# Attending the first and last batch in half-heads, with the half-batch MLPs woven in sooner and q/k loaded apart from v

## The chip, the cores and the metric

One core of a Trainium2 chip runs the kernel. The metric is the device time in microseconds (us) of one execution; "median" is over several executions. The span of a profile runs from the first to the last instruction of the program and is about 1.8 us shorter than the time of the same execution. TensorE is called PE in the profile, VectorE DVE, ScalarE ACT, GpSimd POOL, SyncE SP. SP issues most of the DMAs.

## The reference, cut to what matters

Hashed attention over 4 batches, 8 heads, 768 positions, 64 features, followed by an MLP:

```python
q_bits = einsum('bhsd,dk->bhsk', q, proj) > 0      # 6 bits; k_bits likewise
mask   = bucket(q_bits)[..., :, None] == bucket(k_bits)[..., None, :]
scores = where(mask, q @ k.T / sqrt(64), -1e9)
attn   = softmax(scores)
x      = (attn @ v).transpose(0, 2, 1, 3).reshape(3072, 512)
h      = x @ w_in                  # 512 -> 2048
out    = (h * cos(h)) @ w_out      # 2048 -> 512
```

The kernel puts 6 features of +0.5 or -0.5 for the hash bits behind the 64 features of q and k, so that one matmul gives score and mask together, and the exp of a score with differing bits vanishes.

## The kernel before

A *slot* is one head. In slot `hd`, nine *units* run; each makes 512 of the 4608 score columns of head `hd` and a ninth of the attention of head `hd - 1`. Between the units stand the preparation of later heads and, from slot 12 on, the MLP of a finished batch.

```python
for hd in range(NH + 1):
    for i in WEIGHTS.get(hd, ()):
        load_weight(i)                       # POOL issues; 16 loads in slots 3 to 12
    if hd in MLP_AT:                         # {12: 0, 20: 1, 28: 2}
        for c in range(2):
            hidden(MLP_AT[hd], c, wide)      # x @ w_in, sin on ACT, product on DVE
    for u in range(NU):                      # NU = 9
        scores(hd, u)                        # PE, then exp on ACT
        attend(hd - 1, u * NA, (u + 1) * NA) # PE
        ...                                  # project(): pieces of g @ w_out; plan: preparation
    normalize(hd - 1)                        # DVE: reciprocal and product into xtok
    if hd % H == 0:
        for t in range(SB):
            to_features(hd // H - 1, t)      # SP: DMA transpose of xtok into xT
...                                          # tail: rest of batch 2's MLP, the whole of batch 3's
```

Preparing a head takes a load of q, k and v (SP, two heads at a time), six transposes (PE) with two evictions, two casts to bf16 (DVE), and the hash: a matmul with `proj` for up to four heads at once, a threshold on DVE, and two small DMAs per head that place the bits in the rows behind the features. In the profile's lines `nat` (later `nat_qk` and `nat_v`) is a loaded pair, `ext` the features with their bits, `xtok` the attention's result, `xT` the same transposed, `win` and `wout` the two weight matrices, and the `L` number a line of that run's kernel.

```python
def place_bits(heads, bits):
    for j, hd in enumerate(heads):
        for r in range(2):
            a = 32 * j + r * NBITS
            nc.sync.dma_start(out=e_all[D:KEXT, hd % NE, :, r * HB:(r + 1) * HB],
                              in_=bits[a:a + NBITS])
...
for m in range(4, NH // 2):
    at(2 * m - 7, 2, load_pair, m)           # slot, unit: load of heads 2m, 2m+1
...
    if hd % GH == GH - 2 and hd + 2 < NH and hd > 2:
        hash_at(hd, 5, list(range(hd + 2, hd + 2 + GH)))   # then place_bits of four heads
```

The softmax here doesn't subtract the row's maximum and nothing guards it: scores larger than these inputs give would overflow.

## Time and profile before

| | before |
|---|---|
| time, median (runs) | 335.7 us (335.0 to 336.5, 4 runs) |
| span of the profile | 333.1 us |
| TensorE work, back to back (worked out below) | 302.9 us |
| first exp / first hidden layer / last exp ends | 10.7 / 75.9 / 276.5 us |
| ACT table loads | 8 of 1.28 us |

The page's first two parts: busy time of each engine, and the span in 40 slices of 8.3 us (a digit is the busy share in tenths; PEclk is the granted TensorE clock).

```profile
PE 320.3 (96%) x2794; PEld 193.6 (58%) x2794; DVE 175.8 (53%) x346; ACT 243.6 (73%) x453; POOL 82.4 (25%) x219
...
PE   7889999799999999999999999999999999999995
...
ACT  3677989689788768869778868869878882577211
...
PEclk9999999799999999999999999999999999999999
DMA  7943784999601405565000515341000003500021
```

PE is the limit, but its busy share does not say by how much, because the record of a matmul overlaps those of its neighbours (a record of 512 columns lasts 378 ns, and the next matmul starts after 216). So I took for each shape of matmul the usual distance from one start to the next in dense stretches (512 columns 216 ns, 384 columns 162 ns, 65-column attend about 30 ns, fp32 transpose 109 ns, a pass of a hash group 330 ns) and added these up. That gives 302.9 us of work; the other 30.2 us of the span are lost. They lie as follows, by the start of each reciprocal, which ends a slot: 12.3 us up to the end of slot 6, at 49.2 us; 6.3 us in slots 7 to 11; 7.6 us from there to the end of attention; 4.1 us in the tail. The split is good to about 1 us: a second working, with slightly different spacings, gave 13.1, 6.4, 6.3 and 4.2 us.

The one large hole is near 60 us. The windows view gives busy time in chosen stretches: length, then PE, weight loads, DVE, ACT, POOL, with the granted clock, the DMA share and GB/s last.

```profile
core 0: us, PE busy (x) PEld busy (x) DVE busy (x) ACT busy (x) POOL busy (x), PEclk, DMA share, GB/s
...
46.00:53.00 7.00, 7.00 (x88) 4.41 (x87) 4.43 (x9) 5.99 (x13) 3.28 (x10) 1.00 0.44 88
53.00:62.00 9.00, 6.89 (x85) 5.00 (x83) 5.20 (x11) 7.70 (x16) 5.41 (x14) 1.00 0.80 195
62.00:66.30 4.30, 4.08 (x34) 2.90 (x35) 0.76 (x3) 2.60 (x5) 0.28 (x1) 0.60 1.78 174
66.30:76.00 9.70, 9.70 (x126) 6.59 (x125) 6.72 (x13) 8.57 (x18) 7.26 (x17) 1.00 0.91 204
```

PE stands for 2 us before 62 us, and then runs at 0.60 of its clock in the mean. What it waits for is the first row of the next answer (waits view: who waited for whom, total us, times, longest):

```profile
PE tp L123 <- DMA nat<-in_k_dram: 2.3, 1, 2.3
```

And this is why that load came late (timeline of SP's queue: start, length, operation):

```profile
37.35 0.41 SPq L82 DMA_DIRECT2D nat<-in_q_dram  x1
...
49.00 6.24 SPq L169 DMA_DIRECT2D ext<-bits  x8
55.36 0.37 SPq L82 DMA_DIRECT2D nat<-in_q_dram  x1
```

The eight bit placements of one hash group hold SP for 6.24 us, 0.78 us each, and the load of pair 7 stands behind them in program order.

### The profile page before, as it was taken

How to read it: one execution, taken by the hardware profiler on the slowest of the kernel's cores; microseconds unless marked ns; L12 is line 12 of the kernel's file. 1: busy time of each engine (PE TensorE's matmuls, PEld its weight loads, DVE VectorE, ACT ScalarE, POOL GpSimd, SP SyncE). 2: the span in 40 equal slices, each digit the busy share in tenths (PEclk: the TensorE clock that was granted, in tenths of full speed). 3: DMA queues.
4: the chain of work that ended last, by engine and by line, in shares of the span. 5: the costliest groups of instructions: out<-in, count | busy, mean ns of one | idle time of the engine just before them, and what ended most of it. 6: DMA issues, size and time to landing. Idle time of an engine off the chain costs nothing.

```text
span 333.1 us, 7151 instructions
## 1 busy us (share of the span) xinstructions
PE 320.3 (96%) x2794; PEld 193.6 (58%) x2794; DVE 175.8 (53%) x346; ACT 243.6 (73%) x453; POOL 82.4 (25%) x219
## 2 busy tenths in 40 slices
PE   7889999799999999999999999999999999999995
PEld 2466767565666566656666656656565565566442
DVE  6787766376884444554885444352983101188100
ACT  3677989689788768869778868869878882577211
POOL 9993645376002223222002222221000000000000
PEclk9999999799999999999999999999999999999999
DMA  7943784999601405565000515341000003500021
GB/s 209 321 136 91 175 242 100 210 224 179 177 3 38 148 31 176 96 211 174 6 1 2 175 36 176 69 94 43 0 1 2 33 31 81 143 2 1 33 94 63
DMA packets 34398, 33.55 MB, mean 101 GB/s; under 512 B 15060, under 2 KB 30396, under 8 KB 34364
## 3 DMA queue, kind: packets, MB, share of 16 engines
q1 hardware_dynamic: 30732, 28.76, 29.5%
q0 software_dynamic: 3328, 4.20, 8.1%
q8 instruction: 22, 0.36, 0.5%
q10 hardware_dynamic: 304, 0.13, 0.1%
q14 instruction: 12, 0.10, 0.1%
HBM read 27.27 MB, written 6.29 MB: 101 GB/s over the span
## 4 chain that ended last, share of the span: by engine, by line
PE 82%; ACT 7%; DVE 4%; DMA 3%; issue 3%; POOL 1%; SPq 0%; ACTq 0%; DVEq 0%
PE y L307 18%; PE st L201 16%; PE st L283 13%; PE o_att L283 9%; PE o_att L230 9%; PE tp L307 6%; PE tp L123 5%; ACT pt L209 5%; PE tp L155 4%; DMA nat<-in_k_dram 3%; DVE ext L142 1%; PE o_att L220 1%; ACT o_sb L322 1%; DVE ext L147 1%; ACT L291 1%
## 5 line engine op out<-in xcount | busy, mean ns | idle before, releaser
L209 ACT ACTIVATE pt<-st 128x512 f16<-128x512 f32 x288 | 158.8, 610 | 37.1 <-PE st L201 35.2
L201 PE MATMUL st<-ext 128*128 128x512 bf16 (+1 forms) x384 | 108.2, 328 | 1.5 <-ACT pt L209 1.3
L230 PEld LDWEIGHTS <-pt 128*128 128x128 f16 x1152 | 72.3, 98 | 39.1 <-issue 1.4
L307 PE MATMUL y<-wout,gt 128*128 128x512 f16 x288 | 89.3, 378 | 0.8
L230 PE MATMUL o_att<-v_ext,pt 128*128 128x65 f16 x1152 | 82.7, 195 | 0.3 <-ACT pt L209 0.3
L107 POOL CAST v_ext<-nat 128x192 f16<-128x192 f32 x64 | 21.8, 368 | 138.4 <-PE o_att L230 135.9
L201 PEld LDWEIGHTS <-ext 128*128 128x128 bf16 x384 | 36.8, 98 | 23.6 <-issue 10.6
L295 DVE TENSOR_TENSOR gt<-st,cs 128x384 f16<-128x384 f32 x76 | 41.9, 556 | 5.5
L291 ACT ACTIVATE cs<-st 128x384 f16<-128x384 f32 x76 | 37.2, 491 | 9.7 <-PE st L283 9.5
L307 PEld LDWEIGHTS <-gt 128*128 128x128 f16 x384 | 33.1, 98 | 18.2 <-issue 1.4
L295 DVE TENSOR_TENSOR gt<-o_att,cs 128x384 f16<-128x384 f32 x52 | 28.9, 557 | 21.2 <-ACT cs L291 17.8
L244 DVE RECIPROCAL rec<-o_att 128x6 f32<-128x6 f32 x32 | 6.3, 196 | 62.7 <-PE o_att L230 62.7
L123 PE MATMUL tp<-ident,nat 128*128 128x128 f32 x186 | 31.9, 282 | 3.9 <-DMA nat<-in_k_dram 2.3
L291 ACT ACTIVATE cs<-o_att 128x384 f16<-128x384 f32 x52 | 25.6, 492 | 6.4 <-PE o_att L283 6.3
L123 PEld LDWEIGHTS tp<-ident,nat 128*128 128x128 f32 x186 | 22.3, 143 | 9.9 <-issue 3.6
L283 PE MATMUL st<-xT,win_100 128*128 128x384 f16 x76 | 24.8, 326 | 0.0
L283 PE MATMUL st<-xT,win_101 128*128 128x384 f16 x76 | 24.8, 326 | 0.0
L283 PE MATMUL st<-xT,win_102 128*128 128x384 f16 x76 | 24.8, 326 | 0.0
L283 PE MATMUL st<-xT,win_103 128*128 128x384 f16 x76 | 24.8, 326 | 0.0
L307 PE MATMUL tp<-wout,gt 128*128 128x512 f16 x96 | 21.2, 379 | 0.0
L111 POOL TENSOR_TENSOR vacc<-nat 128x192 f32<-128x192 f32 x32 | 18.8, 589 | 0.0
L245 DVE TENSOR_TENSOR xtok<-o_att,rec 128x384 f16<-128x384 f32 x32 | 17.8, 557 | 1.6 <-DMA xT<-xtok 0.5
(173 smaller groups left out, 358.0 us busy)
## 6 DMA issues: line engine op xcount, KB each, us to landing
out_dram<-o_sb SPq DMA_DIRECT2D x23, 256.0 KB
nat<-in_q_dram SPq DMA_DIRECT2D x15, 384.0 KB
nat<-in_k_dram SPq DMA_DIRECT2D x15, 384.0 KB
nat<-in_v_dram SPq DMA_DIRECT2D x15, 384.0 KB
wout<-in_moe_w_out_dram POOLq DMA_DIRECT2D x8, 256.0 KB, 8.4
ext<-bits SPq DMA_DIRECT2D x62, 9.0 KB
win_100<-in_moe_w_in_dram POOLq DMA_DIRECT2D x2, 256.0 KB, 4.2
win_101<-in_moe_w_in_dram POOLq DMA_DIRECT2D x2, 256.0 KB, 6.8
```

The costliest lines, as they stand in the source:

```text
L107: nc.gpsimd.tensor_copy(out=dst[:, r], in_=src[:, r])
L111: nc.gpsimd.tensor_add(acc, x[:, 0:3 * D], x[:, 3 * D:6 * D])
L123: nc.tensor.matmul(out=tp[:, i * P:(i + 1) * P], lhsT=nat[hd][:, w, i * 2 * D:(i + 1) * 2 * D], rhs=ident, is_transpose=True, start=(i == ...
L155: nc.tensor.matmul(out=jp[32 * j:32 * (j + 1), 0:HB], lhsT=projx, rhs=f32[hd][:, w], start=True, stop=True,)
L201: nc.tensor.matmul(out=st[:, o:o + n], lhsT=e[:, 1, jt * P:(jt + 1) * P], rhs=e[:, 0, c:c + n], start=True, stop=True,)
L209: nc.scalar.activation(out=pts[hd][:, u * UNIT:(u + 1) * UNIT], in_=st, func=ACTF.Exp, bias=EXP_BIAS, scale=EXP_SCALE,)
L230: nc.tensor.matmul(out=o_ps[:, qt * VW:(qt + 1) * VW], lhsT=pts[hd][:, jt * S + qt * P:jt * S + (qt + 1) * P], rhs=v_all[:, hd % NV, jt], ...
L245: nc.vector.tensor_tensor(out=xtok[b][:, :, h * D:(h + 1) * D], in0=o_ps[:, :, 0:D], in1=rec.to_broadcast([P, SB, D]), op=ALU.mult,)
L283: nc.tensor.matmul(out=hp[:, 0:TOK], lhsT=win_t[ft][:, ff * P:(ff + 1) * P], rhs=xT[:, ft, b * S + c * TOK:b * S + (c + 1) * TOK], start=( ...
L291: nc.scalar.activation(out=cs, in_=hp[:, 0:TOK], func=ACTF.Sin, bias=math.pi / 2.0, scale=1.0)
L295: nc.vector.tensor_tensor(out=gt, in0=hp[:, 0:TOK], in1=cs, op=ALU.mult)
L307: nc.tensor.matmul(out=y_state[b, t], lhsT=gates[b, c][ff][:, tt * P:(tt + 1) * P], rhs=wout_t[:, ff], start=(ff == 0), stop=(ff == NFF - 1),)
```

## The change

Batch 0 and batch 3 are attended in half-heads: a slot then holds the even query rows of two heads instead of all rows of one. After five slots the even rows of all heads of batch 0 are done, so half a batch can go through the MLP: the first hidden layer moves from slot 12 to slot 7. In batch 3 the first half-batch is woven into the attention, and a shorter MLP is left at the end. q and k have a load and four buffers of their own, v another. The scores use the 70 filled rows and no longer the zeroed 128. The core of the diff, cut:

```diff
+    SLOTS = []
+    for b in range(B):
+        if 0 < b < B - 1:
+            SLOTS += [[(b * H + i, 0, SB)] for i in range(H)]
+        else:
+            first = [(b * H + i, 0, NQ) for i in range(H)]
+            rest = [(b * H + i, NQ, NQ) for i in range(H)]
+            if b == 0:
+                first.insert(1, rest.pop(0))
+            halves = first + rest
+            SLOTS += [halves[i:i + 2] for i in range(0, 2 * H, 2)]
...
-    MLP_AT = {12: 0, 20: 1, 28: 2}
...
+    hiddens.update({7: [(0, 0)], 10: [(0, 1)], 18: [(1, 0)], 19: [(1, 1)], 26: [(2, 0)], 27: [(2, 1)], 30: [(3, 0)]})
+    spread([(0, t) for t in range(SB)], 7, 18)
...
-        load_pair(0, 1)
+        load_qk(0, 1)
...
+        load_qk(1)
+        load_v(0)
+        load_qk(2)
+        load_v(1)
...
-    WEIGHTS = {3 + i: (i,) for i in range(8)}
-    WEIGHTS.update({11: (8, 9), 12: (10, 11, 12, 13, 14, 15)})
...
+    for i in range(8):
+        at(1.4 + 0.4 * i, load_weight, i)
+        at(5 + 0.25 * i, load_weight, 8 + i)
...
-    both(1, 2, transpose, 4)
...
+    hash_at(1.6, [4, 5])
...
+    hash_at(2.5, [6, 7])
...
+                if s == 5:
+                    attend(4, min(2 * u * NA, SB * SB), min(2 * (u + 1) * NA, SB * SB))
...
+                if s == 5 and u == SB * SB // (2 * NA):
+                    normalize(4)
+                    for t in range(NQ):
+                        to_features(0, t)
```

The last two pieces attend slot 4 at double pace inside slot 5 and then transpose the first half-batch by DMA, so that `xT` is there for the hidden layer of slot 7. The second weight matrix (`load_weight` 8 to 15, the tile `wout`) is asked for from slot 5 on.

More of the change, by code (lines that the diff above doesn't have):

```diff
@@ L53 @@
     NU = SB * S // UNIT
+    NQ = SB // 2
+    TOK = S // 2
     glob = ctx.enter_context(tc.tile_pool(name="glob", bufs=1))
     ROW = [2 * (t % (SB // 2)) + t // (SB // 2) for t in range(SB)]
-    p_nat = ctx.enter_context(tc.tile_pool(name="p_nat", bufs=3))
+    p_nat = ctx.enter_context(tc.tile_pool(name="p_nat", bufs=4))
     p_f32 = ctx.enter_context(tc.tile_pool(name="p_f32", bufs=6))
@@ L63 @@
     p_pt = ctx.enter_context(tc.tile_pool(name="p_pt", bufs=2))
-    p_vs = ctx.enter_context(tc.tile_pool(name="p_vs", bufs=7))
+    p_vs = ctx.enter_context(tc.tile_pool(name="p_vs", bufs=4))
+    p_xt = ctx.enter_context(tc.tile_pool(name="p_xt", bufs=4))
     p_x = ctx.enter_context(tc.tile_pool(name="p_x", bufs=2))
@@ L72, with load_qk @@
     ps_y = ctx.enter_context(tc.tile_pool(name="ps_y", bufs=1, space=PSUM))
-    nat, f32, vsum, pts, xtok = {}, {}, {}, {}, {}
-    def load_pair(m, heads=2):
+    nat, nat_v, f32, pts, xtok, xT, held = {}, {}, {}, {}, {}, {}, {}
+    def load_qk(m, heads=2):
         b, h = divmod(2 * m, H)
-        t = p_nat.tile([P, 2, 3, SB * D], FP32, name="nat")
+        t = p_nat.tile([P, 2, 2, SB * D], FP32, name="nat_qk")
         for i in range(0, 2, heads):
-            for w, x in enumerate((q, k, v)):
+            for w, x in enumerate((q, k)):
                 nc.sync.dma_start(
@@ L85, in load_pair, with load_v @@
                 )
-            nat[2 * m + i] = t[:, i]
-            nat[2 * m + i + heads - 1] = t[:, i + heads - 1]
+        nat[2 * m], nat[2 * m + 1] = t[:, 0], t[:, 1]
+    def load_v(m):
+        b, h = divmod(2 * m, H)
+        t = p_nat.tile([P, 2, SB * D], FP32, name="nat_v")
+        nc.sync.dma_start(out=t, in_=v[b, h:h + 2].rearrange("h (p t) d -> p h (t d)", t=SB))
+        nat_v[2 * m], nat_v[2 * m + 1] = t[:, 0], t[:, 1]
     ident = glob.tile([P, P], FP32)
@@ L93 @@
     wout_t = glob.tile([P, NFF, D_MODEL], FP16, name="wout")
-    xT = glob.tile([P, NFT, N_TOK], FP16)
-    NV = 6
-    v_all = glob.tile([P, NV, SB, VW], FP16, name="v_ext")
+    NV = 10
+    v_all = glob.tile([P, NV, SB + 1, VW], FP16, name="v_ext")
     NE = 8
@@ L103, in cast_v @@
     def cast_v(hd):
-        src = nat[hd][:, 2].rearrange("p (t r d) -> p r t d", r=2, d=D)
-        dst = v_all[:, hd % NV, :, 0:D].rearrange("p (r t) d -> p r t d", r=2)
+        held["v", hd % NV] = hd
+        src = nat_v[hd].rearrange("p (t r d) -> p r t d", r=2, d=D)
+        dst = v_all[:, hd % NV, 0:SB, 0:D].rearrange("p (r t) d -> p r t d", r=2)
         for r in range(2):
@@ L108, in cast_v @@
         acc = p_vs.tile([P, 3 * D], FP32, name="vacc")
-        vs = p_vs.tile([P, VW], FP16, name="vs")
-        x = nat[hd][:, 2]
+        x = nat_v[hd]
         nc.gpsimd.tensor_add(acc, x[:, 0:3 * D], x[:, 3 * D:6 * D])
         nc.gpsimd.tensor_add(acc[:, 0:D], acc[:, 0:D], acc[:, D:2 * D])
-        nc.gpsimd.tensor_add(vs[:, 0:D], acc[:, 0:D], acc[:, 2 * D:3 * D])
-        nc.gpsimd.memset(vs[:, D:VW], float(SB))
-        vsum[hd] = vs
+        nc.gpsimd.tensor_add(v_all[:, hd % NV, SB, 0:D], acc[:, 0:D], acc[:, 2 * D:3 * D])
     def transpose(hd, w, engine="dve", pool=None, name="tp"):
@@ L136, in cast @@
     def cast(hd, r, engine="dve"):
+        held[r, hd % NE] = hd
         out_ap = e_all[0:D, hd % NE, :, r * HB:(r + 1) * HB]
@@ L166, in place_bits @@
         for j, hd in enumerate(heads):
+            held["bits", hd % NE] = hd
             for r in range(2):
@@ L184, in hash_direct, with place_direct, scores @@
             )
-        for r in range(2):
-            threshold(
-                e_all[D:KEXT, hd % NE, w, r * HB:(r + 1) * HB],
-                jp[32 * r:32 * r + NBITS, 0:HB],
-            )
-    def scores(hd, u):
-        e = e_all[:, hd % NE]
+        return jp
+    def place_direct(hd, w, r, jp):
+        held["bits", hd % NE] = hd
+        threshold(
+            e_all[D:KEXT, hd % NE, w, r * HB:(r + 1) * HB],
+            jp[32 * r:32 * r + NBITS, 0:HB],
+        )
+    def scores(s, u):
         if u == 0:
-            pts[hd] = p_pt.tile([P, SB * S], FP16, name="pt")
+            pts[s] = p_pt.tile([P, NU * UNIT], FP16, name="pt")
         st = ps_st.tile([P, UNIT], FP32, name="st", space=PSUM)
-        f0 = u * UNIT
-        while f0 < (u + 1) * UNIT:
-            jt, c = divmod(f0, S)
-            n = min(S - c, (u + 1) * UNIT - f0)
-            o = f0 - u * UNIT
+        f = u * UNIT
+        while f < (u + 1) * UNIT:
+            part, g = divmod(f, NU * UNIT // len(SLOTS[s]))
+            hd, t0, nt = SLOTS[s][part]
+            jt, c = divmod(g, nt * P)
+            n = min(nt * P - c, (u + 1) * UNIT - f)
+            o = f - u * UNIT
+            e = e_all[0:KEXT, hd % NE]
+            assert all(held[x, hd % NE] == hd for x in (0, 1, "bits"))
             nc.tensor.matmul(
@@ L203, in scores @@
                 lhsT=e[:, 1, jt * P:(jt + 1) * P],
-                rhs=e[:, 0, c:c + n],
+                rhs=e[:, 0, t0 * P + c:t0 * P + c + n],
                 start=True,
@@ L207, in scores @@
             )
-            f0 += n
+            f += n
         nc.scalar.activation(
-            out=pts[hd][:, u * UNIT:(u + 1) * UNIT], in_=st, func=ACTF.Exp,
+            out=pts[s][:, u * UNIT:(u + 1) * UNIT], in_=st, func=ACTF.Exp,
             bias=EXP_BIAS, scale=EXP_SCALE,
@@ L214, with attend @@
     o_state = {}
-    def attend(hd, i0, i1):
+    def attend(s, i0, i1):
         if i0 == 0:
-            o_ps = ps_o.tile([P, 512], FP32, name="o_att", space=PSUM)
-            o_state[hd] = o_ps
-            nc.tensor.matmul(
-                out=o_ps[:, 0:SB * VW].rearrange("p (t d) -> p t d", d=VW),
-                lhsT=delta,
-                rhs=vsum.pop(hd)[:, None, :].to_broadcast([P, SB, VW]),
-                start=True,
-                stop=False,
-            )
-        o_ps = o_state[hd]
+            o_state[s] = ps_o.tile([P, 512], FP32, name="o_att", space=PSUM)
+            o = 0
+            for hd, t0, nt in SLOTS[s]:
+                nc.tensor.matmul(
+                    out=o_state[s][:, o:o + nt * VW].rearrange("p (t d) -> p t d", d=VW),
+                    lhsT=delta,
+                    rhs=v_all[:, hd % NV, SB, None, :].to_broadcast([P, nt, VW]),
+                    start=(o == 0),
+                    stop=False,
+                )
+                o += nt * VW
         for i in range(i0, i1):
             qt, jt = divmod(i, SB)
+            part, tl = divmod(qt, SB // len(SLOTS[s]))
+            hd, t0, nt = SLOTS[s][part]
+            assert held["v", hd % NV] == hd
+            f = (part * SB + jt) * nt * P + tl * P
             nc.tensor.matmul(
-                out=o_ps[:, qt * VW:(qt + 1) * VW],
-                lhsT=pts[hd][:, jt * S + qt * P:jt * S + (qt + 1) * P],
+                out=o_state[s][:, qt * VW:(qt + 1) * VW],
+                lhsT=pts[s][:, f:f + P],
                 rhs=v_all[:, hd % NV, jt],
@@ L236, in attend, with normalize @@
             )
-    def normalize(hd):
-        b, h = divmod(hd, H)
-        o_ps = o_state.pop(hd)[:, 0:SB * VW].rearrange("p (t d) -> p t d", d=VW)
-        if h == 0:
-            xtok[b] = p_x.tile([P, SB, D_MODEL], FP16, name="xtok")
+    def normalize(s):
+        o_ps = o_state.pop(s)[:, 0:SB * VW].rearrange("p (t d) -> p t d", d=VW)
         rec = p_vs.tile([P, SB, 1], FP32, name="rec")
         nc.vector.reciprocal(out=rec, in_=o_ps[:, :, D:VW])
-        nc.vector.tensor_tensor(
-            out=xtok[b][:, :, h * D:(h + 1) * D],
-            in0=o_ps[:, :, 0:D],
-            in1=rec.to_broadcast([P, SB, D]),
-            op=ALU.mult,
-        )
+        o = 0
+        for hd, t0, nt in SLOTS[s]:
+            b, h = divmod(hd, H)
+            if b not in xtok:
+                xtok[b] = p_x.tile([P, SB, D_MODEL], FP16, name="xtok")
+            nc.vector.tensor_tensor(
+                out=xtok[b][:, t0:t0 + nt, h * D:(h + 1) * D],
+                in0=o_ps[:, o:o + nt, 0:D],
+                in1=rec[:, o:o + nt].to_broadcast([P, nt, D]),
+                op=ALU.mult,
+            )
+            o += nt
     def to_features(b, t):
+        c, tt = divmod(t, NQ)
+        if tt == 0:
+            xT[b, c] = p_xt.tile([P, NFT, TOK], FP16, name="xT")
         nc.sync.dma_start_transpose(
-            out=xT[:, :, b * S + t * P:b * S + (t + 1) * P], in_=xtok[b][:, t, :]
+            out=xT[b, c][:, :, tt * P:(tt + 1) * P], in_=xtok[b][:, t, :]
         )
@@ L272 @@
     out_v = out.rearrange("(b p t) m -> b t p m", b=B, t=SB)
-    TOK = S // 2
     gates = {}
@@ L285, in hidden @@
                     lhsT=win_t[ft][:, ff * P:(ff + 1) * P],
-                    rhs=xT[:, ft, b * S + c * TOK:b * S + (c + 1) * TOK],
+                    rhs=xT[b, c][:, ft],
                     start=(ft == 0),
@@ L327, in emit_out, with when, at, hash_at @@
             )
-    AHEAD = GH + 1
-    NA = SB * SB // NU
-    MLP_AT = {12: 0, 20: 1, 28: 2}
-    BRIDGE = 3
-    fill = {}
-    for start, b in MLP_AT.items():
-        for t in range(SB if b < B - 2 else SB - BRIDGE):
-            f0 = 0
-            for i in range(NU + 3):
-                n = 0 if i == NU + 2 else 2 - i % 2 if i < NU + 1 else 1
-                slot, u = divmod((start * NU) + t * (NU + 3) + i, NU)
-                if slot >= NH:
-                    slot, u, n = NH - 1, NU - 1, NFF - f0
-                if n:
-                    fill.setdefault((slot, u), []).append((b, t, f0, f0 + n))
-                    f0 += n
-    WEIGHTS = {3 + i: (i,) for i in range(8)}
-    WEIGHTS.update({11: (8, 9), 12: (10, 11, 12, 13, 14, 15)})
-    wide = [(ps_o, "o_att"), (ps_st, "st"), (ps_o, "o_att"), (ps_st, "st"), (ps_st, "st")]
-    plan = {}
-    def at(slot, u, f, *args):
-        plan.setdefault((slot, u), []).append((f, args))
-    def hash_at(slot, u, heads):
+    SLOTS = []
[9 more added lines that the diff above has]
+            SLOTS += [halves[i:i + 2] for i in range(0, 2 * H, 2)]
+    NS = len(SLOTS)
+    NA = SB * SB // NU
+    wide = [(ps_o, "o_att"), (ps_st, "st"), (ps_o, "o_att"), (ps_st, "st"), (ps_st, "st")]
+    plan, fill, hiddens, features = {}, {}, {}, {}
+    def when(time):
+        return int(round(time * NU))
+    def at(time, f, *args):
+        plan.setdefault(when(time), []).append((f, args))
+    def hash_at(time, heads, gap=1 / 9):
         bits = []
@@ L364, in second @@
             place_bits(heads, bits[0])
-        at(slot, u, first)
-        at(slot, u + 1, second)
-    def both(slot, u, f, hd):
-        at(slot, u, f, hd, 0)
-        at(slot, u + 1, f, hd, 1)
-    at(0, 0, cast_v, 2)
-    at(0, 4, cast_v, 3)
-    at(0, 1, load_pair, 3)
-    at(1, 3, cast_v, 4)
-    at(1, 7, cast_v, 5)
-    at(2, 3, cast_v, 6)
-    at(3, 3, cast_v, 7)
-    for m in range(4, NH // 2):
-        at(2 * m - 7, 2, load_pair, m)
-    for hd in range(4, NH - 4):
-        at(hd, 4, cast_v, hd + 4)
@@ L384 @@
-    both(0, 1, transpose, 2)
-    both(0, 3, cast, 1)
-    both(0, 5, transpose, 3)
-    both(0, 6, cast, 2)
-    hash_at(1, 0, [2, 3])
-    both(1, 2, transpose, 4)
-    both(1, 3, cast, 3)
-    both(1, 5, transpose, 5)
-    both(1, 7, cast, 4)
-    both(2, 0, transpose, 6)
-    both(2, 2, transpose, 7)
-    hash_at(2, 4, list(range(GH, 2 * GH)))
-    both(2, 6, cast, 5)
-    both(3, 4, cast, 6)
-    for hd in range(3, NH):
-        if hd + GH < NH:
-            both(hd, 1, cast, hd + GH)
-        if hd + AHEAD < NH:
-            at(hd, 0, transpose, hd + AHEAD, 0)
-            at(hd, 3, transpose, hd + AHEAD, 1)
-        if hd % GH == GH - 2 and hd + 2 < NH and hd > 2:
-            hash_at(hd, 5, list(range(hd + 2, hd + 2 + GH)))
+        at(time, first)
@@ new lines, in hash_at, with both, spread @@
+        at(time + gap, second)
+    def both(time, f, hd, gap=1 / 9):
+        at(time, f, hd, 0)
+        at(time + gap, f, hd, 1)
+    def spread(tiles, s0, s1):
+        total = (s1 - s0) * NU
+        for k, (b, t) in enumerate(tiles):
+            a, z = k * total // len(tiles), (k + 1) * total // len(tiles) - 1
+            for i in range(a, z):
+                f0, f1 = ((j - a) * NFF // (z - a) for j in (i, i + 1))
+                if f1 > f0:
+                    fill.setdefault(s0 * NU + i, []).append((b, t, f0, f1))
@@ new lines @@
+    hiddens.update({7: [(0, 0)], 10: [(0, 1)], 18: [(1, 0)], 19: [(1, 1)], 26: [(2, 0)], 27: [(2, 1)], 30: [(3, 0)]})
+    spread([(0, t) for t in range(SB)], 7, 18)
+    spread([(1, t) for t in range(SB)], 18, 26)
+    spread([(2, t) for t in range(SB)], 26, NS)
+    features.update({8: (0, 1), 16: (1, None), 24: (2, None), 28: (3, 0), 32: (3, 1)})
+    both(0, transpose, 2)
+    both(0.3, transpose, 3)
+    at(0.4, cast, 1, 0)
+    at(0.5, cast, 1, 1)
+    hash_at(0.6, [2, 3])
+    at(0.8, cast, 2, 0)
@@ new lines @@
+    both(0.9, transpose, 4)
+    at(1.0, cast, 2, 1)
+    both(1.2, transpose, 5)
+    at(1.3, cast, 3, 0)
+    at(1.4, cast, 3, 1)
+    hash_at(1.6, [4, 5])
+    both(1.8, cast, 4)
+    both(2.1, transpose, 6)
+    both(2.25, transpose, 7)
+    both(2.7, cast, 5)
+    hash_at(2.5, [6, 7])
+    both(3.0, cast, 6)
+    both(3.4, cast, 7)
+    CAST = {8: 4.5, 9: 6.0, 10: 6.5, 11: 7.5, 12: 8.5, 13: 9.5, 14: 10.3}
+    CAST.update({hd: 11.1 + 0.8 * (hd - 15) for hd in range(15, 30)})
+    CAST.update({30: 23.25, 31: 24.12})
@@ new lines, with free @@
+    for hd, c in CAST.items():
+        both(c - 2 if hd > 10 else c - 1, transpose, hd, 0.25)
+        both(c, cast, hd)
+    hash_at(7, [8, 9, 10, 11])
+    for heads, time in (
+        ((12, 13, 14, 15), 9.7), ((16, 17, 18, 19), 13), ((20, 21, 22, 23), 17.2),
+        ((24, 25, 26, 27), 20), ((28, 29), 22.9), ((30, 31), 25.2),
+    ):
+        hash_at(time, heads)
+    def free(hd):
+        return hd // 2 + 6 if 0 < hd < H else hd + 2
+    for hd in range(1, NH):
+        at(max(CAST[hd] - 1.9, free(hd - NV) if hd >= NV else 0) if hd >= H else 0.4 * (hd - 1), cast_v, hd)
@@ L407 @@
+    at(0, load_qk, 3)
+    at(0, load_v, 2)
+    at(0.3, load_v, 3)
+    at(2.2, load_qk, 4)
+    at(2.2, load_v, 4)
+    for m in range(5, NH // 2):
+        at(CAST[2 * m] - 3.7, load_qk, m)
+        at(CAST[2 * m] - 3.5, load_v, m)
+    for i in range(8):
+        at(1.4 + 0.4 * i, load_weight, i)
+        at(5 + 0.25 * i, load_weight, 8 + i)
     with tc.manual_schedule():
@@ L416 @@
         nc.scalar.activation(out=once, in_=warm, func=ACTF.Exp)
-        load_pair(1)
-        load_pair(2)
-        nc.vector.memset(v_all[:, :, :, D:VW], 1.0)
+        load_qk(1)
+        load_v(0)
+        load_qk(2)
+        load_v(1)
+        nc.vector.memset(v_all[:, :, 0:SB, D:VW], 1.0)
+        nc.vector.memset(v_all[:, :, SB, D:VW], float(SB))
         nc.vector.memset(delta, DELTA)
-        for i in range(NE):
-            (nc.vector if i < 3 else nc.gpsimd).memset(e_all[D:P, i], 0.0)
         wp = ps_y.tile([P, 512], FP32, name="y", space=PSUM)
@@ L429 @@
         transpose(0, 1)
+        jq = hash_direct(0, 0)
+        jk = hash_direct(0, 1)
         cast(0, 0)
         cast(0, 1, "act")
-        hash_direct(0, 0)
-        hash_direct(0, 1)
+        place_direct(0, 0, 0, jq)
+        place_direct(0, 1, 0, jk)
+        place_direct(0, 1, 1, jk)
+        place_direct(0, 0, 1, jq)
         transpose(1, 0, "act", ps_o, "o_att")
@@ L440 @@
         cast_v(0)
-        cast_v(1)
-        for hd in range(NH + 1):
-            for i in WEIGHTS.get(hd, ()):
-                load_weight(i)
-            if hd in MLP_AT:
-                for c in range(2):
-                    hidden(MLP_AT[hd], c, wide)
-            for u in range(NU):
-                if hd < NH:
-                    scores(hd, u)
-                if hd > 0:
-                    attend(hd - 1, u * NA, (u + 1) * NA)
-                for b, t, f0, f1 in fill.get((hd, u), ()):
+        for s in range(NS + 1):
+            for b, c in hiddens.get(s, ()):
+                hidden(b, c, wide)
+            for u in range(NU):
+                now = s * NU + u
+                if s < NS:
+                    scores(s, u)
+                if s == 5:
+                    attend(4, min(2 * u * NA, SB * SB), min(2 * (u + 1) * NA, SB * SB))
+                elif s > 0:
+                    attend(s - 1, u * NA, (u + 1) * NA)
+                for b, t, f0, f1 in fill.get(now, ()):
@@ L455 @@
                     project(b, t, f0, f1)
-                for f, args in plan.get((hd, u), ()):
+                for f, args in plan.get(now, ()):
                     f(*args)
-                for b, t, f0, f1 in fill.get((hd, u), ()):
+                for b, t, f0, f1 in fill.get(now, ()):
                     if f1 == NFF:
                         emit_out(b, t, "act")
-            if hd > 0:
-                normalize(hd - 1)
-                if hd % H == 0:
-                    for t in range(SB):
-                        to_features(hd // H - 1, t)
@@ L467 @@
-        ys = [(ps_y, "y"), (ps_t, "tp"), (ps_t, "tp")]
-        for t in range(SB - BRIDGE, SB):
-            project(B - 2, t, 0, NFF, *ys[t % 3])
-            emit_out(B - 2, t, "act")
-        for c in range(2):
-            hidden(B - 1, c, wide)
-        for t in range(SB):
+                if s == 5 and u == SB * SB // (2 * NA):
+                    normalize(4)
+                    for t in range(NQ):
+                        to_features(0, t)
+            if s > 0:
+                if s != 5:
+                    normalize(s - 1)
+                if s in features:
+                    b, c = features[s]
+                    for t in range(SB) if c is None else range(c * NQ, (c + 1) * NQ):
+                        to_features(b, t)
@@ L474 @@
+        ys = [(ps_y, "y"), (ps_t, "tp"), (ps_t, "tp")]
+        for t in range(NQ):
+            project(B - 1, t, 0, NFF, *ys[t % 3])
+            emit_out(B - 1, t, "act")
+        hidden(B - 1, 1, wide)
+        for t in range(NQ, SB):
             project(B - 1, t, 0, NFF, *ys[t % 3])
```

## The prediction

> **What bounds it now.** TensorE. The page's busy line has PE 96%, ACT 73%, DVE 53%. I summed start-to-start spacings from the timeline (512 columns 216 ns, 384 columns 162 ns, 128x65 attend 29 to 32 ns, fp32 transpose 109 ns, one hash pass 330 ns): about 303 us of back-to-back work in a span of 333 us. So 30 us at most, and early. Between two reciprocals (one head slot) in 76 to 277 us only 0.1 to 0.5 us is lost; after 277 us only the 3.9 us drain. Before 76 us about 19 us are lost:
> - 0 to 10.3 us: about 6 us (head 0's k lands at 4.4 us, then a 1.41 us cast and four 0.55 us thresholds; head 1's k lands at 8.06 us).
> - slots 1 and 2 take 6.5 us each: DVE is nearly full.
> - slots without MLP are bound by ACT: nine exps at 0.47 us are 4.24 us, TensorE has 3.8 us.
> - at 58 to 66 us a late load of pair 7 (behind eight bit placements on SP) stops TensorE for 2.5 us; afterwards the granted clock is 0.50 for 3.4 us (0.79 mean in the windows view). Cost 4.4 us. The Trainium skill ("TensorE: Matmul & The Clock Gate", the HAM clock gate) says an idle window halves the clock; the trace agrees.
>
> **What the change does.**
> - Batch 0's MLP begins in slot 7 instead of 12 (about 46 us instead of 76). Slots 7 to 11 become TensorE-bound, and separate q/k loads with four buffers remove the 58 us stall: 6.3 us of loss there shrink to about 1.5. Gain 4 to 5 us.
> - Prologue: without v ahead, head 1's k lands about 1.2 us sooner; POOL's memsets beside DVE's cast vanish; the first scores need two thresholds, not four. First score near 9.1 us instead of 10.3. Slots 0 to 4 now need two heads each, so DVE stays the limit and bit placements come close to their use: gain 1 to 2 us in all.
> - Added: two more hash groups, 1.33 us of TensorE each, 2.7 us. Hidden layers enter ACT seven times instead of three before the tail: eight more table loads (1.28 us each), mostly hidden, 1 to 2 us of TensorE. 96 more score matmuls for the same columns: 0.2 us.
> - K of the scores falls from 128 to 70 rows: no change; the same skill page (LDWEIGHTS) says time goes with columns.
> - Last batch in halves: attention with MLP is already TensorE-bound there; no gain.
>
> Net about -2 to -7 us, all before 76 us. Predicted **331 us**, range **326 to 336.5**. Faster by over 2%: 0.38; within 2%: 0.58; slower: 0.04.
>
> **Checks in the profile.** No half clock or load wait near 60 us; first exp near 9.5 us; first sin table load near 46 us; later slots as tight as now; drain unchanged; tail after the last exp 31 us instead of 56; 15 to 16 table loads.
>
> **What would make it wrong.** Weights (8.4 MB read) must land by about 50 us beside seven pairs: DMA share, 0.6 to 0.9 before, would be near 1, and a late weight stalls the first hidden layer (slower). Late bits in slots 1 to 4 cost 1 to 3 us each. If slots 0 to 6 run at ACT's pace (4.3 us), slot 7 starts at 40 us and the time falls to 326 us or less.

## The result

| | before | changed |
|---|---|---|
| time, median | 335.7 us (335.0 to 336.5, 4 runs) | 349.3 us (348.5 to 350.0, 4 runs) |
| ratio, 95% interval | | 1.040 (1.036 to 1.045) |
| span of the profile, clock | 333.1 us, 0.993 | 346.7 us, 0.98 |
| TensorE work / lost | 302.9 / 30.2 us | 305.8 / 40.9 us |
| end of slot 6 | 49.2 us | 53.3 us |
| first exp / first hidden layer / last exp ends | 10.7 / 75.9 / 276.5 us | 9.9 / 62.0 / 311.1 us |

A ratio here and below is the mean time of one kernel's fast runs over that of the fast runs of before in the same rounds, so it is not quite the ratio of the medians. Executions over 1.5% slower than the fastest of the same kernel are left out of the means.

The change made the kernel 4% slower. The 13.6 us between the spans are accounted for in this way (each is a difference of lost time in a stage, from the reciprocals and the sums of spacings; the second working moves single figures by about 1 us, but the differences between the kernels by only about 0.2 us):

| stage | lost before | lost after |
|---|---|---|
| start to end of slot 6 | 12.3 us | 15.8 us |
| slots 7 to 11 before; slot 7 after | 6.3 us | 11.3 us |
| to the end of attention | 7.6 us | 9.7 us |
| tail | 4.1 us | 4.1 us |
| work | 302.9 us | 305.8 us |

The same parts of the page for the changed kernel:

```profile
PE 325.7 (94%) x2906; PEld 200.5 (58%) x2906; DVE 175.8 (51%) x364; ACT 254.7 (73%) x461; POOL 75.8 (22%) x182
...
PE   8977991899999999999999999999999999999995
...
ACT  4756893378789878878888688788898888871731
...
PEclk9999897699999999999999999999999999999999
DMA  7938999501903432464500510023000030013001
```

The seventh slice of PE has sunk to a tenth, and PEclk shows 7 and 6 there and in the next slice. The windows of the same stretches as before:

```profile
46.00:53.00 7.00, 6.91 (x87) 5.66 (x84) 5.81 (x13) 6.41 (x14) 6.84 (x13) 1.00 1.18 202
53.00:62.00 9.00, 0.16 (x5) 0.05 (x2) 1.13 (x4) 2.14 (x3) 3.32 (x10) 0.67 1.23 202
62.00:66.30 4.30, 4.29 (x14) 2.02 (x15) 1.12 (x2) 1.24 (x3) 0.00 (x0) 0.50 0.69 232
66.30:76.00 9.70, 9.70 (x69) 5.57 (x66) 7.82 (x14) 7.40 (x15) 0.00 (x0) 1.00 0.00 0
```

From 53 to 62 us PE does next to nothing (0.16 us), while the DMA engines are full. Then it runs at half its clock until 66.3 us. The waits view names what it waited for:

```profile
PE o_att L308 <- DMA xT<-xtok: 8.9, 1, 8.9
...
PE st L214 <- DMA ext<-bits: 4.0, 2, 2.4
```

L308 is the first hidden layer, L214 the scores. The chain that ended last passes through the same two kinds of DMA (start, length, what):

```profile
14.79 4.51 DMA ext<-bits
...
30.30 4.41 DMA ext<-bits
...
48.23 1.33 SPq L279
49.56 0.05 issue
49.62 12.30 DMA xT<-xtok
61.92 0.09 issue
62.01 1.44 PE o_att L308 x4
```

So there are two things to explain: a transpose that takes 12.3 us from its issue to the wait it ends, and bit placements that end waits near 19 and 35 us. Beside the transposes POOL was issuing the loads of the second weight matrix (timeline of POOL):

```profile
44.81 2.89 POOL L292 DMA_DIRECT2D wout<-in_moe_w_out_dram  x4
...
49.84 2.88 POOL L292 DMA_DIRECT2D wout<-in_moe_w_out_dram  x4
```

In the trace's DMA packets, the three transposes are 1536 packets of 256 bytes. The first starts at 50.8 us and the last at 61.2 us. In that time 1603 packets of the weights' queue start, nearly all of 1 KB and about 99 ns each, while a transpose packet takes 33 ns. The DMA view of the stretch from 50 to 61 us shows the two queues (packets, MB, share of 16 engines):

```profile
q0 software_dynamic: 1758, 1.70, 93.8%
q1 hardware_dynamic: 1642, 0.42, 30.4%
```

The Trainium skill says in "DMA: Bandwidth & Descriptors" (Queues, rings and completion order) that each DMA engine goes round-robin between the queues that have work, packet by packet. The trace agrees in its counts: 1536 beside 1603 in all, and in each microsecond from 51 to 60 us 136 to 194 transpose packets beside 123 to 158 of the weights. It doesn't keep which engine a packet ran on or whether its packets are those of the page, so the alternation itself isn't seen. If the turns are equal, a transfer made of small packets gets half of the turns but a small part of the bytes: here 0.4 MB beside 1.7 MB. My estimate from these numbers: 1536 packets over 16 engines are 96 on each, in 10.4 us one per 108 ns, about the time of a weight packet.

### The profile page after: what moved, and what is told of

The parts are those of the page before. It is cut to its first block, busy times and chain, and to the rows that moved or that the text cites. A ratio compares the mean times of both kernels' runs of the same rounds, so it can differ in the third digit from the quotient of the medians.

```text
span 346.7 us, 7362 instructions
## 1 busy us (share of the span) xinstructions
PE 325.7 (94%) x2906; PEld 200.5 (58%) x2906; DVE 175.8 (51%) x364; ACT 254.7 (73%) x461; POOL 75.8 (22%) x182
## 4 chain that ended last, share of the span: by engine, by line
PE 87%; DMA 6%; DVE 4%; ACT 2%; SPq 0%; issue 0%; DVEq 0%
PE y L332 20%; PE st L214 17%; PE st L308 15%; PE o_att L308 10%; PE o_att L249 10%; PE tp L128 5%; PE tp L161 4%; PE tp L332 4%; DMA xT<-xtok 4%; DMA ext<-bits 3%; PE o_att L235 1%; ACT pt L222 1%; DVE ext L148 1%; DVE qk L139 1%; PE y L484 1%; DVE bits L153 1%
## 5 line engine op out<-in xcount | busy, mean ns | idle before, releaser
L214 PE MATMUL st<-ext 70*128 70x512 bf16 (+3 forms) x480 | 110.0, 296 | 4.7 <-DMA ext<-bits 4.0
L308 PEld LDWEIGHTS <-win 128*128 128x128 f16 x512 | 50.4, 99 | 43.7 <-issue 11.8
L214 PEld LDWEIGHTS <-ext 70*128 70x128 bf16 x480 | 43.9, 98 | 40.7 <-issue 14.4
L308 PE MATMUL st<-xT,win 128*128 128x384 f16 x304 | 58.8, 329 | 0.0
L139 DVE COPY qk<-tp 128x384 f32<-128x384 f32 x61 | 33.6, 557 | 49.5 <-PE tp L128 49.2
L115 POOL CAST v_ext<-nat_v 128x192 f16<-128x192 f32 x64 | 22.3, 378 | 136.6 <-PE o_att L249 90.1
L308 PE MATMUL o_att<-xT,win 128*128 128x384 f16 x208 | 43.6, 333 | 8.9 <-DMA xT<-xtok 8.9
L148 DVE TENSOR_SCALAR ext<-qk 64x768 bf16<-64x768 f32 x63 | 37.7, 598 | 1.0
L128 PE MATMUL tp<-ident,nat_qk 128*128 128x128 f32 x186 | 31.9, 284 | 1.0 <-DVE qk L139 0.9
L128 PEld LDWEIGHTS tp<-ident,nat_qk 128*128 128x128 f32 x186 | 23.0, 144 | 6.6 <-DVE qk L139 1.7
```

What stands on the lines that cost most here:

```text
L115: nc.gpsimd.tensor_copy(out=dst[:, r], in_=src[:, r])
L128: nc.tensor.matmul(out=tp[:, i * P:(i + 1) * P], lhsT=nat[hd][:, w, i * 2 * D:(i + 1) * 2 * D], rhs=ident, is_transpose=True, start=(i == ...
L139: nc.vector.tensor_copy(out=f32[hd][:, w], in_=tp[:, 0:HB])
L148: nc.vector.tensor_scalar(out=out_ap, in0=in_ap, scalar1=QK_PRESCALE, scalar2=None, op0=ALU.mult,)
L214: nc.tensor.matmul(out=st[:, o:o + n], lhsT=e[:, 1, jt * P:(jt + 1) * P], rhs=e[:, 0, t0 * P + c:t0 * P + c + n], start=True, stop=True,)
L308: nc.tensor.matmul(out=hp[:, 0:TOK], lhsT=win_t[ft][:, ff * P:(ff + 1) * P], rhs=xT[b, c][:, ft], start=(ft == 0), stop=(ft == NFT - 1),)
```

## The experiments

Theory W says that the weights' packets make the transposes slow, and with them the first hidden layer. Its rival L says that three transposes take 12 us anyway. About the early slots, theory P says that half-heads from slot 1 on want two new heads per slot, faster than DVE and the way of the bits through a DMA can give them; its rivals blame the DMA traffic in front of the bits, or the half-heads in themselves.

| run | what | median (range), us | ratio to before, 95% |
|---|---|---|---|
| a1 | changed, second weight matrix later | 339.0 (338.6 to 342.3) | 1.013 (1.006 to 1.020) |
| a2 | changed, MLP two slots later | 349.1 (347.7 to 349.8) | 1.039 (1.034 to 1.044) |
| a3 | changed, dummy matmuls in the wait | 348.5 (345.5 to 349.0) | 1.036 (1.030 to 1.042) |
| a5 | a1, pair 4 loaded sooner | 337.7 (336.8 to 342.7) | 1.007 (1.004 to 1.011) |
| a6 | a5, pair 3 behind the first bits | 344.3 (340.4 to 347.5) | 1.024 (1.017 to 1.031) |
| a7 | a1, last batch in whole heads | 340.6 (340.5 to 343.1) | 1.019 (1.015 to 1.023) |
| a8 | heads 0 to 3 whole, 4 to 7 in halves | 335.9 (335.6 to 340.1) | 1.006 (0.997 to 1.014) |
| a9 | a8, hash groups of four | 340.9 (340.6 to 343.6) | 1.018 (1.012 to 1.025) |
| a10 | a8, second matrix between a8's and the old place | 334.7 (331.9 to 339.2) | 0.990 (0.981 to 0.999) |
| a11 | a10, second matrix waits for xT | 332.3 (331.7 to 332.6) | 0.989 (0.986 to 0.993) |
| b1 | before, loads apart | 337.6 (335.8 to 339.4) | 1.001 (0.994 to 1.009) |
| b3 | before, pair loaded before the bits | 330.4 (329.8 to 331.3) | 0.984 (0.980 to 0.988) |
| b5 | b3 with the change's prologue | 330.2 (329.5 to 330.8) | 0.986 (0.983 to 0.989) |

All were correct. There were four executions of each (six of a11). One of a5, a6 and a10 each, the profiled one, was slow; medians and ranges include it, ratios don't.

### a1: the second weight matrix later

```diff
-        at(5 + 0.25 * i, load_weight, 8 + i)
+        at(62 / 9, load_weight, 8 + i)       # behind cast_v(12) on POOL, also moved to 62 / 9
```

> The changed kernel, but the eight loads of the second weight matrix are issued only after the POOL cast of head 12, at about 53 us, so none of them shares the DMA engines with the three transposes into xT that the first hidden layer waits for. Theory W (the transposes' 256-byte packets alternated with the 1 KB weight packets): the transposes land about 4 to 5 us after the last is issued, the 8.9 us wait on xT shrinks below 1.5 us, no half clock between 56 and 66 us, time 337 to 340 us. Rival L (three transposes take 12 us by themselves, and the schedule just gave them too little): the wait stays near 9 us, time 347 us or more.

The time is 339.0 us, as W had it. The 1536 transpose packets ran from 49.3 to 52.7 us, in 3.4 us instead of 10.4, at 21 ns each; L falls. The DMA view from 49 to 53 us and the window that had been empty:

```profile
q1 hardware_dynamic: 1632, 0.39, 55.5%
q0 software_dynamic: 18, 0.03, 4.1%
```

```profile
53.00:62.00 9.00, 9.00 (x69) 5.73 (x67) 6.89 (x16) 8.30 (x17) 8.61 (x16) 1.00 1.06 239
```

Slot 7 now loses 0.7 us instead of 11.3. The kernel is still 1.3% slower than before; slot 6 ends at 54.5 us.

### a2: the MLP two slots later

```diff
-    hiddens.update({7: [(0, 0)], 10: [(0, 1)], ...
-    spread([(0, t) for t in range(SB)], 7, 18)
+    hiddens.update({9: [(0, 0)], 11: [(0, 1)], ...
+    spread([(0, t) for t in range(SB)], 9, 18)
```

> The changed kernel with the first hidden layer in slot 9 instead of 7; all loads stay. W and L both: two ACT-bound slots (about 4.3 us each) run while the transposes land, the wait on xT and the half clock after it vanish; 11 us of loss go, about 1 to 1.5 us of ACT-bound loss come back: 338 to 341 us. If instead the early slots are starved by the weights themselves, slots 7 and 8 are much longer than 4.5 us and the time stays above 344 us.

This was a miss: 349.1 us. Giving the transposes two more slots did not help. They also held up what was queued behind them, as I read the order in the trace; no run tests that apart. The wait moved from the hidden layer to the scores of slot 8 (timeline of all engines):

```profile
50.67 0.58 SPq L85 DMA_DIRECT2D nat_qk<-in_q_dram  x1
...
55.18 12.75 SPq L176 DMA_DIRECT2D ext<-bits  x8
...
67.16 0.10 PEld L214 LDWEIGHTS <-ext 70*128 70x128 bf16 x1 [9.47 <-DMA ext<-bits]
67.19 0.58 PE L214 MATMUL st<-ext 70*128 70x512 bf16 x1 [9.38 <-DMA ext<-bits]
```

(The first of these rows is from the timeline of SP alone.) The transposes were issued at 45.7 to 48.5 us and their packets ended at 60.9 us; behind them in SP's queue came pair 6 and then the bits of head 8, which landed at 67 us. So it was slot 8 that starved, and not for weights, as the alternative in the expectation had it, but for bits that waited in line.

### a3: dummy matmuls through the wait

```diff
+                if s == 7:
+                    wq = ps_y.tile([P, 512], FP32, name="y", space=PSUM)
+                    for _ in range(40):
+                        nc.tensor.matmul(out=wq[0:1], lhsT=warm, rhs=warm.to_broadcast([P, 512]), start=True, stop=True)
```

> The changed kernel with forty 512-column matmuls on a dummy tile just before the first hidden layer, so that TensorE is busy through the wait on xT. The wait itself stays (hidden layer at 62 us). If the half clock after the wait costs what the trace shows (matmuls at 320 instead of 162 ns until 66.3 us), the time falls by about 2 us to 347 us; if the clock record means nothing for the time, it stays at 349 us.

Inconclusive. The clock stayed full through the hidden layer, and the median fell by 0.8 us, but the intervals overlap (1.030 to 1.042 against 1.036 to 1.045), and in the profiled execution an earlier wait was 1.8 us longer than in the changed kernel's. In its trace slot 7 loses 9.3 us instead of 11.3, so the half clock after the wait is a matter of 2 us, not of the 13 us.

### b3 and b1: the hole of the kernel before

b3 changes one line, so that from pair 5 on a load stands in front of the hash group's placements; b1 gives q/k and v their own four buffers and leaves every load in its place.

```diff
-        at(2 * m - 7, 2, load_pair, m)
+        at(*((2 * m - 8, 5) if m > 4 else (1, 2)), load_pair, m)
```

> The kernel before, with one line changed: from pair 5 on a pair is loaded 6 units sooner, in front of the eight bit placements of the hash group on the SP queue. Theory: the 58 us stall is the SP queue's order, pair 7 lands about 6 us sooner, the 2.5 us wait and the half clock after it vanish: 331 to 332.5 us. Rival (the buffer, freed late by the POOL cast, or DMA share makes the load late): no change, 335 to 336 us.

> The kernel before with q/k and v in separate tiles of four buffers each (xT holds two batches, for the room), every load at its old place in the program. If the buffers were what made pair 7 late, as the prediction had it in part, 331 to 332 us as in b3; if only its place behind the eight bit placements in the SP queue was, no change: 335 to 336 us, with the wait near 60 us still there.

b3 takes 330.4 us, b1 is level with before. It was the place in SP's queue, not the buffers: in b1 pair 7 is still issued at 55.6 us, as the eight placements end. b1's own trace is of one of its two executions near 339 us (the other two took 335.8 and 335.9). In it PE waits only 1.6 us for pair 7, without a half clock, but 4.3 us near 75 us for a later pair, which had stood behind six transposes that held SP for 9.4 us. Pair 7 is now issued 16 us sooner, not 6 (timeline of SP in b3):

```profile
39.31 0.37 SPq L82 DMA_DIRECT2D nat<-in_q_dram  x1
...
48.29 6.13 SPq L169 DMA_DIRECT2D ext<-bits  x8
```

and the windows have no hole and no half clock:

```profile
53.00:62.00 9.00, 9.00 (x117) 6.72 (x114) 5.88 (x13) 9.00 (x20) 5.56 (x15) 1.00 0.89 200
62.00:66.30 4.30, 4.30 (x59) 2.62 (x55) 2.93 (x6) 3.92 (x8) 3.03 (x7) 1.00 1.35 99
```

### a5 and a6: what stands in front of the bits

```diff
-    at(2.2, load_qk, 4)                      # a5, and load_v(4) with it
+    at(1.0, load_qk, 4)
-    at(0, load_qk, 3)                        # a6 as well, with load_v(2), load_v(3)
+    at(0.8, load_qk, 3)
```

> The kernel with the late second weight matrix (a1), and pair 4 loaded at slot 1.0 instead of 2.2, so that it moves while the DMA engines are nearly idle (18 to 28 us) and not just ahead of the bits of heads 6 and 7. Theory F (the bit placements wait in the one queue of SP behind data that was issued first): the wait of 3.2 us near 33 us, and the half clock after it, go; 334 to 336 us. Rival D (the bits are late because DVE makes them late, at 30.3 us): the wait stays within 1 us of 3.2 us and the time at 338 to 339 us.

> As a5, and also v of pair 2 and all of pair 3 are issued after the bits of heads 2 and 3 instead of before them. Theory F: the wait of about 2 us near 18 us on these bits goes as well, 1 to 2 us below a5, unless the later v of pair 2 holds up POOL (then the first attends wait and it is no faster than a5). Rival D: as a5.

a5 came to 336.8 to 338.3 us in its fast runs, 0.5% below a1 by the ratios (the intervals overlap), and not at the 334 to 336 us of theory F. a6 was worse than a5. So the data in front of the bits is a small part of their lateness at most. The profiled executions of both were slow ones, so I don't read more from them.

### a7: the last batch in whole heads

```diff
-        if 0 < b < B - 1:
+        if 0 < b:
...                                           # hidden(3, *) after the attention, two tiles of batch 2 as bridge
```

> As a1, but the last batch is attended in whole heads, its MLP comes wholly after the attention, and two tiles of batch 2 bridge to it. The prediction said that the half-heads of the last batch gain nothing because TensorE is the limit there anyway: 338 to 340 us, as a1 (339.0). If weaving the half-batch MLP in sooner is worth what the change meant it to be, 342 us or more.

340.6 us, 0.6% above a1; the intervals overlap. In the traces, one of each, from 228 us on a1 loses 5.9 us and a7 7.6 us. Half-heads in the last batch are worth 1 to 2 us here, if anything; the prediction said that they gain nothing.

### a8: half-heads only where the heads are ready

```diff
-            if b == 0:
-                first.insert(1, rest.pop(0))
             halves = first + rest
+            if b == 0:
+                halves = [x for p in zip(first[:4], rest[:4]) for x in p] + first[4:] + rest[4:]
...                                           # first hidden layer in slot 8; w_out behind cast_v(14)
```

> The changed kernel with the late second weight matrix, but in batch 0 heads 0 to 3 are attended whole and only heads 4 to 7 in halves; the first half-batch is complete one slot later, so its hidden layer comes in slot 8. Two new heads per slot are then wanted only in slots 4 and 5 instead of 1 to 4. Theory P (half-heads from slot 1 on use heads faster than DVE and the 4.4 us way of their bits through a DMA can prepare them): the waits on bits near 18 and 33 us vanish, slot 7 ends near 53 us as in b3, time 331 to 333.5 us against 339 for a1. Rival (half-heads cost in themselves, through more and smaller score matmuls, two hash groups and more table loads): 337 us or more.

The waits on bits are gone from the waits view, and slot 7 ends at 53.1 us, where a1 ended slot 6 only at 54.5. That is what P had forecast (near 53 us), and it speaks against the half-heads in themselves. By the times alone a8 is not clear of a1 (the intervals overlap); a11 below is. The time, 335.9 us, missed P's 331 to 333.5 by a fault of mine: the cast of head 14 waited for its own v until 57 us and held back the second matrix (timeline of PE):

```profile
64.42 0.38 PE L332 MATMUL y<-wout,gt 128*128 128x512 f16 x1 [0.58 <-DMA wout<-in_moe_w_out_dram]
...
67.57 0.38 PE L332 MATMUL y<-wout,gt 128*128 128x512 f16 x1 [1.85 <-DMA wout<-in_moe_w_out_dram]
```

### a9: hash groups of four

```diff
-    hash_at(1.6, [4, 5])
-    hash_at(2.5, [6, 7])
+    hash_at(2.5, [4, 5, 6, 7])               # and 28 to 31 in one group at slot 24
```

> As a8, with heads 4 to 7 hashed in one group and heads 28 to 31 in one group again: 2.66 us of TensorE work less (1.33 us a group). If TensorE bounds it as the sums say, the group of 28 to 31 gives its 1.3 us in full and that of 4 to 7 nothing to 1.3 us (slots there are bound by ACT): 1.3 to 2.7 us below a8, so 329 to 331.5 us, level with b3 (330.4) or just below it.

A clear miss: 5 us slower than a8 though it has 2.66 us less to do. A group of four heads is eight placements at once, and they again stood in front of a load, that of pair 5 (timelines of SP and of PE):

```profile
26.75 6.15 SPq L176 DMA_DIRECT2D ext<-bits  x8
33.01 0.38 SPq L85 DMA_DIRECT2D nat_qk<-in_q_dram  x1
...
34.51 0.41 SPq L85 DMA_DIRECT2D nat_qk<-in_q_dram  x1
```

```profile
47.75 0.87 PE L128 MATMUL tp<-ident,nat_qk 128*128 128x128 f32 x3 [4.26 <-DMA nat_qk<-in_q_dram]
```

The load that PE then waited for is not that one but the next, pair 6. It was issued at 34.5 us, no later than in a8 (34.3 us), but by the chain that ended last it took 13.1 us: pair 5 had come 2 us later than in a8, and five loads of the first weight matrix were issued from 33.5 to 37.6 us beside the two pairs, where a8 issued its five from 36.8 us on. A hidden layer near 229 us also waited 2.3 us for its xT; there the eight placements (216.6 to 222.9 us) stood in front of the six transposes, which began 5.8 us later than in a8, 3.2 us of it lag from the early slots. So the change's pairs were no mere cost of TensorE work, as the prediction booked them; they also kept the queue short.

### a10 and a11: the race between weights and transposes

a10 puts the second matrix behind the cast of head 13 instead of 14. a11 adds one copy:

```diff
+    def after_xT():
+        held_up = glob.tile([P, 1], FP16, name="held_up")
+        nc.gpsimd.tensor_copy(out=held_up, in_=xT[0, 0][:, 0, TOK - 1:TOK])
+
+    at(71 / 9, after_xT)                      # in front of load_weight 8 to 15
```

> As a8, with the eight loads of the second weight matrix issued behind the POOL cast of head 13 (about 50 us) and not behind that of head 14, whose own load held them up until 59 us: they start as the transposes end, and the projections of slot 8 find their weights. The 2.8 us of waits near 64 us and the half clock after them (4.7 us lost in slot 8, against 0.7 in a1) go: 331 to 333 us. If they overlap the transposes again, the first hidden layer waits instead and it stays at 335 to 336 us.

> As a10, but a one-column POOL copy out of the last transposed tile stands in front of the loads of the second weight matrix, so that none of them can be issued before the transposes have landed, however the execution falls. a10 scattered between 331.9 and 339.2 us, and its profiled execution waited 5.1 us for xT. If that scatter is the race between the weight packets and the transposes, all fast executions come out at 331 to 333 us with less than 0.5 us of waiting for xT. If it is something else, the scatter of several us stays.

a10 scattered over 7 us (4.6 us in its three fast runs); in its profiled execution, the slow one, the first hidden layer waited 5.0 us. With the dependency all six executions of a11 lie between 331.7 and 332.6 us, and its trace shows no such wait. That points to the race, that is, to which of the two transfers gets going first. It is not a clean proof of the scatter, since the two rounds ran on different chips and the kernel before itself scattered over 4.6 us in a10's round and 3.0 in a11's. POOL waits in PE's place, and PE's own wait for the late matrix is 0.4 us (waits view; then the window):

```profile
POOL held_up L463 <- DMA xT<-xtok: 2.5, 1, 2.5
```

```profile
53.00:62.00 9.00, 9.00 (x57) 5.43 (x56) 7.06 (x17) 7.79 (x16) 7.27 (x14) 1.00 1.14 243
```

The first hidden layer starts at 52.6 us, and slot 8 loses 0.9 us.

### b5: the prologue alone

```diff
-        load_pair(0, 1)
+        load_qk(0, 1)
...                                           # memsets of e_all gone, e_all[0:KEXT], hash before cast
```

> The kernel before with the order fix (b3) and only the change's prologue: q and k loaded ahead of v in buffers of their own, scores over 70 rows without the memsets of the padding, the first head hashed before it is cast; heads and MLP stay as before. The first score was at about 9.3 us in the changed kernel and 10.3 us in the one before: 329 to 330 us, 0.5 to 1.5 us below b3 (330.4). If the rows or the memsets mattered more, below 328.5 us.

330.2 us, level with b3 (0.986 against 0.984). The first exp starts at 9.9 us instead of 10.7, and the first hidden layer at 70.8 instead of 71.5, but the end of the last exp is the same, 272.1 us. In dense stretches a 512-column score matmul over 70 rows follows the one before it after 219 ns, over 128 rows after 215 ns, and the slots from 71 us on are each about 0.03 us longer (0.7 us over 21 slots). That would use up the lead; I did not test it apart.

## Why the prediction was wrong, point by point

- **"Batch 0's MLP begins in slot 7 instead of 12 (about 46 us instead of 76) ... 6.3 us of loss there shrink to about 1.5. Gain 4 to 5 us."** This step failed. The hidden layer began at 62.0 us, and slot 7 alone lost 11.3 us. I had asked whether the weights would land in time, and not what they would do to another transfer: the transposes took 10.4 us beside the weight packets and 3.4 us without them (a1). The mechanism is shown by a1 and a11. With the race closed and the early slots eased, the hidden layer comes at 52.6 us and the slot loses 0.9 us (a11), so the size I gave the gain was about right for a schedule that the change did not have.
- **"Slots 0 to 4 now need two heads each ... gain 1 to 2 us in all."** This failed too. Slot 6 ended 4.1 us later than before instead of 3 us sooner, with 0.6 us more work done by then. "Late bits in slots 1 to 4 cost 1 to 3 us each" stood among the risks, and that is what happened: PE stood 1.6 and 2.4 us for bits, and the clock was at half from 35.6 to 39.0 us. Easing the demand removes both waits (a8); moving the data in front of the bits hardly does (a5). The 4.4 to 4.5 us in the chain from a threshold to the score it frees is the number that I should have set against the slot.
- **"separate q/k loads with four buffers remove the 58 us stall"**. The stall was rightly found, and rightly put down to the eight placements on SP, but buffers alone don't gain anything (b1: 1.001). The order does (b3: 0.984). In the changed kernel it gave way to the larger wait at the same place.
- **"two more hash groups ... 2.7 us"** and the total of work were right: the same sum over the changed trace gives 305.8 us, 2.9 us more. a9 shows that taking the groups back would have cost more.
- **"Hidden layers enter ACT seven times ... 1 to 2 us"**: sixteen table loads, as foretold; the loss from slot 8 or 12 to the end of attention grew by 2.1 us, all causes together.
- **"Last batch in halves ... no gain"**: 1 to 2 us of gain (a7), too small to matter.
- **"First score near 9.1 us"**: 9.4 us, first exp at 9.9. Right in kind; b5 shows that alone it does not shorten the kernel.
- **"K of the scores falls from 128 to 70 rows: no change"**: nearly. The spacing of a 512-column score matmul grew from 215 to 219 ns (b5), which is small beside the rest.
- **The checks.** "No half clock or load wait near 60 us" failed: the clock was at half from 56.1 to 66.3 us. The first sin table load came at 53.9 us, not near 46, and the tail after the last exp took 35.6 us, not 31. The drain of 3.9 us after the last matmul did not change, as foretold.

In sum the forecast of 331 us went wrong by 18 us: 7 us in slots 0 to 6, 10 us at the first hidden layer, and 1 to 2 us after. Still open is how the early 7 us split between the way of the bits, the DVE and the half clock; a8 only shows that together they hang on the demand for two heads per slot.

The fastest kernels found are not the changed one: the kernel before with one load moved in front of eight small ones takes 330.4 us (330.2 us with the prologue), 1.6% less than before. The half-heads, with their two faults mended (a11), come to 332.3 us, 1.1% less; the intervals of b3 and a11 overlap.

## What to carry to other kernels

When work is moved sooner, list the DMAs in flight at the new time and ask which of them are made of small packets: here 256-byte packets beside 1 KB ones took 10.4 us for what takes 3.4 us without them, and what stood behind them in the same queue came late too (a2). Put the loads that nobody needs yet behind a data dependency on the transfer that somebody waits for; a place in the program alone leaves a race, and scatter from execution to execution (a10) can be its sign. Before adding buffers for a late load, look at what its issuing queue was doing before it.

## What the Trainium skill lacked or had wrong

- "DMA: Bandwidth & Descriptors" (Queues, rings and completion order) has the round-robin by packet, but not what follows for transfers of unlike packets: 1536 packets of 256 bytes took 10.4 us beside 1603 packets of mostly 1 KB, and 3.4 us alone.
- The same page (DMA Transpose) has no time for a transpose from SBUF to SBUF under traffic, and doesn't warn that it can hold up what is issued behind it: in a2 the bits of head 8, behind the transposes and a load, kept PE waiting for 9.4 us.
- The same page (Issuing engines are not separate DMA queues) says that the time to initiate a DMA "is usually small relative to the DMA itself". For small DMAs that did not hold here: each placement of 9 KB took SP 0.72 to 0.76 us to issue, and the twelve packets of the first one started within 0.22 us (before, from 50.40 us on); eight of them held SP for 6.24 us and delayed the load behind them; moving that load took 1.6% off the time (b3).
- "TensorE: Matmul & The Clock Gate" (LDWEIGHTS) says that the number of rows doesn't matter for a weight load. For the pairs of weight load and 512-column matmul here, 70 rows were spaced 219 ns and 128 rows 215 ns. The page has no such difference; its cause is open.
- The same page's clock gate has the half clock follow at least one idle window of about 3.4 us. The runs agree in its length, 3.4 us in the kernel before and 10.2 us around the 8.9 us wait of the changed one. But the waits that it followed were shorter than such a window: 2.3 us (before, 62 us), 2.4 us (changed, 35 us) and 1.8 us (a7, 20 us). Waits of 1.6 us (changed, 19 us; b1, 62 us) and 2.0 us (a1, 20 us) were not followed by it.
